# Pooled attention and a gated MLP on one core: the order of all queues made by a list scheduler, and every other early score tile emptied whole

## The chip, the cores and the metric

The kernel runs on one core of a Trainium2 chip. Its time is device microseconds (us) of one execution. The engines are named as the profile names them: PE (matmul; PEld is its weight load), DVE (VectorE), ACT (ScalarE), POOL (GpSimd), SP (the queue that issues all DMAs here). Each engine takes its instructions in the order in which they stand in its queue, and an instruction that waits holds everything behind it on that engine.

## The reference

```python
# q, k, v: (4, 8, 1152, 64) f32;  w_in: (512, 2048), w_out: (2048, 512)
q_pool = q.reshape(B, H, S // 2, 2, D).mean(axis=3)          # 576 pooled queries
scores = matmul(q_pool, k.transpose(0, 1, 3, 2)) / sqrt(D)   # 576 x 1152 per head
attn = exp(scores - max(scores)); attn /= sum(attn) + 1e-9
x = matmul(attn, v)              # -> 2304 tokens x 512
h = x @ w_in
out = (h * clip(h + 3, 0, 6) / 6) @ w_out
```

## The kernel before, in words

**Attention.** The 32 heads are worked in 16 pairs `g`. Of a pair, the pooled queries make 9 score tiles of 128 rows: one that holds the 64 odd rows of both heads, `(None, 0)`, and four per head. Over all there are 144 score tiles `i`. For each tile, `scores` (L229) makes three PSUM tiles `pqk` of 128 x 384 (two matmuls each: an upper and a lower part of q, `qh` and `ql`, against `kT`), and each is emptied by one DVE instruction (L243) that scales it, writes it to the SBUF tile `s` and carries on the running minimum in `cm`. Then `expo` (ACT, L251, 1152 columns, sum in `den`), `recip` (POOL adds eps to `den`, L256; DVE reciprocal, L257), `normal` (POOL, L261, 1152 columns), and `turn` (L263): nine PE transposes into three PSUM tiles `ptp`, each emptied by ACT (L284) or DVE (L282) into `pt`. When the tiles of a row group are turned (5 tiles of 320 columns, then 4 of 256), `values` (L286) multiplies with `vr` into `pav`, and `spill` splits the result into `xh` and `xl` and writes both to DRAM (`xh_d`, `xl_d`).

**Preparation of a pair.** `load_kq`, `load_v`, `pool_q` (L192), `split_k` (L197, L199), `prep_k` (L208, L211, L213), `prep_q` (L221, L226, L227). For pairs after the first, the elementwise part is on POOL.

**Weights.** Of the MLP's weights there are 16 slices `f`, each in two halves (`w_in`, `w_out`). `convert` (L326) rounds a half in seven steps: ACT L331, POOL L332, DVE L334, L338, L341, POOL L344, L345, then a DMA to DRAM (`w_d`, L346). Both halves leave through one staging place, `scratch[:, 0:2]`.

**MLP.** 2304 tokens: six chunks of 256 run among the attention, 16 steps `m` each: `hidden` (12 matmuls `ph`, L88, then L91, L92, L95, L96 on ACT and DVE) and `project` (6 matmuls `po`, L104). Each step loads its slice of the weights from `w_d` again. The last 768 tokens are done behind the attention, as one part of 256 (`mxmxh`, `mxmxl`) and one of 512 (`mxa`, `mxb`): 16 steps of 12 + 6 + 12 + 12 matmuls, the tail.

**What sets the order.** A plan of slots: `at(slot, ...)` files each step under a slot number counted in thirds of a score tile (tile `i` begins in slot 3i; `TRN = 8` slots later it is turned; step `m` of the MLP begins in slot 126 + 6m for the first chunk, then every 2.8 slots). The functions are called in that order, and the framework that turns them into a program lays the instructions of each queue out by an order of its own. PSUM: `pqk` 2 buffers, `ptp` and the other transposes 2, `pav` 1, `ph` 1, `po` 2. The MLP's three buffers are held from the start.

## Time and profile before

| | |
|---|---|
| median of three runs | 1043.81 us (1041.64 to 1047.19) |
| the profiled execution's own time | 1044.61 us |
| its span, first to last instruction | 1042.8 us |
| PE busy | 978.3 us, 94% |
| DVE, ACT, POOL busy | 576.0, 532.3, 426.2 us (55%, 51%, 41%) |
| mean granted TensorE clock | 0.981 |
| DMA | 204 MB, mean 196 GB/s |

A busy PE is an upper bound on its work: matmuls overlap in the array, their ends are modelled, and one that waits for its neighbour looks long. The share is also an average over stages that are limited by different things, so the rows below are taken by stage.

### The profile page before, as it was taken

What the parts mean: (1) busy time and instruction counts of PE and PEld (TensorE: products, weight loads), DVE (VectorE), ACT (ScalarE), POOL (GpSimd) and SP (SyncE); (2) the same over time, 40 slices, a digit from 0 to 9 for tenths busy, and PEclk for the clock granted to TensorE, in tenths of its full rate; (3) what the DMA queues carried; (4) which work ended last, traced back from release to release, by engine and by line L of the source; (5) the groups of instructions that cost most, each with busy time, mean ns of one, the idle gap of its engine ahead of it and who ended that gap; (6) DMA issues with size and microseconds to landing.
All of it is one profiled execution on the core that took longest, in us unless ns stands there. A gap on an engine that the chain in (4) does not pass through costs nothing.

```text
span 1042.8 us, 17686 instructions
## 1 busy us (share of the span) xinstructions
PE 978.3 (94%) x6288; PEld 791.0 (76%) x6288; DVE 576.0 (55%) x1664; ACT 532.3 (51%) x1094; POOL 426.2 (41%) x510
## 2 busy tenths in 40 slices
PE   5797978898899999999999999999999999899997
PEld 3555555566678788888889888888888888688886
DVE  5777666777666656555556554546655454222222
ACT  3555655665465556645556454555555554222222
POOL 4878776878562535342525242342522221000000
PEclk9988989999999999999999999999999999999999
DMA  7665454667754446766767567668656556843332
GB/s 236 207 210 190 171 160 140 214 194 240 235 180 152 154 139 198 226 207 206 262 213 253 183 222 246 199 226 267 225 182 201 194 198 211 298 132 131 122 121 81
DMA packets 80312, 204.06 MB, mean 196 GB/s; under 512 B 7264, under 2 KB 30816, under 8 KB 80224
## 3 DMA queue, kind: packets, MB, share of 16 engines
q1 hardware_dynamic: 80224, 202.93, 59.9%
q8 instruction: 50, 0.82, 0.3%
q14 instruction: 38, 0.31, 0.1%
HBM read 171.97 MB, written 30.93 MB: 195 GB/s over the span
## 4 chain that ended last, share of the span: by engine, by line
PE 76%; POOL 11%; DVE 4%; ACT 3%; issue 2%; DMA 2%; SPq 0%; POOLq 0%; DVEq 0%; ACTq 0%
PE ph L88 18%; PE pqk L239 13%; PE po L104 12%; PE pav L292 12%; PE ptp L269 11%; PE pt L104 6%; POOL s L261 3%; POOL qp L192 2%; POOL scratch L345 2%; PE ptk L208 2%; PE ptq L221 1%; DVE scratch L338 1%; POOL ks L199 1%; DVE s L243 1%; POOL scratch L344 1%
## 5 line engine op out<-in xcount | busy, mean ns | idle before, releaser
L243 DVE TENSOR_SCALAR_CACHE_REDUCE s<-pqk,cm 128x384 f32<-128x384 f32 x288 | 176.5, 613 | 108.0 <-PE pqk L239 105.9
L269 PE MATMUL ptp<-ident,s 128*128 128x128 f32 x1296 | 220.3, 281 | 12.2 <-ACT kT L213 2.2
L261 POOL TENSOR_SCALAR s<-s,den 128x1152 f32<-128x1152 f32 x144 | 181.8, 1263 | 94.6 <-DVE den L257 79.3
L239 PE MATMUL pqk<-kT,qh 128*128 128x384 f32 x480 | 187.4, 406 | 28.1 <-DVE s L243 26.6
L284 ACT COPY pt<-ptp 128x384 f32<-128x384 f32 x314 | 149.0, 480 | 118.4 <-PE ptp L269 113.6
L269 PEld LDWEIGHTS ptp<-ident,s 128*128 128x128 f32 x1296 | 163.9, 144 | 48.4 <-ACT pt L284 9.8
L251 ACT ACTIVATE s<-s,cm 128x1152 f32<-128x1152 f32 x144 | 181.6, 1261 | 27.6 <-DVE s L243 26.5
L88 PE MATMUL ph<-mxmxh,w 128*128 128x256 f32 x896 | 188.6, 292 | 1.1 <-DVE r L92 1.1
L292 PE MATMUL pav<-pt,vr 128*64 128x256 f32 (+1 forms) x1152 | 166.0, 417 | 0.0
L239 PE MATMUL pqk<-kT,ql 128*128 128x384 f32 x480 | 161.7, 353 | 0.0
L256 POOL TENSOR_SCALAR den<-den 128x1 f32<-128x1 f32 x144 | 30.7, 213 | 297.5 <-ACT s L251 291.9
L88 PEld LDWEIGHTS ph<-mxmxh,w 128*128 128x128 f32 x896 | 147.2, 190 | 2.6 <-DVE r L92 1.3
L239 PEld LDWEIGHTS pqk<-kT,qh 128*128 128x128 f32 x480 | 91.4, 197 | 56.3 <-DVE s L243 38.4
L91 ACT ACTIVATE r<-ph,three 128x256 f32<-128x256 f32 (+1 forms) x128 | 63.9, 499 | 133.8 <-PE ph L88 133.6
L88 PE MATMUL ph<-mxmxl,w 128*128 128x256 f32 x448 | 126.9, 283 | 0.0
L292 PEld LDWEIGHTS pav<-pt,vr 128*64 128x64 f32 x1152 | 80.4, 138 | 60.5 <-issue 14.4
L104 PE MATMUL po<-w,gh 128*128 128x512 f32 x384 | 122.8, 397 | 0.0
L92 DVE SCALAR_TENSOR_TENSOR r<-r,ph 128x256 f32<-128x256 f32 (+1 forms) x128 | 57.9, 452 | 111.4 <-ACT r L91 111.2
L243 DVE TENSOR_SCALAR_CACHE_REDUCE s<-pqk 128x384 f32<-128x384 f32 x144 | 79.5, 552 | 41.7 <-PE pqk L239 40.0
L239 PEld LDWEIGHTS pqk<-kT,ql 128*128 128x128 f32 x480 | 94.6, 199 | 2.1
L88 PEld LDWEIGHTS ph<-mxmxl,w 128*128 128x128 f32 x448 | 85.4, 191 | 0.5
L95 ACT CAST gh<-r 128x256 fp32r<-128x256 f32 (+1 forms) x128 | 55.3, 432 | 57.7 <-DVE r L92 56.8
(56 smaller groups left out, 1269.6 us busy)
## 6 DMA issues: line engine op xcount, KB each, us to landing
w<-w_d SPq DMA_DIRECT2D x224, 512.0 KB, 4.7
w_d<-scratch SPq DMA_DIRECT2D x32, 512.0 KB, 3.3
vr<-in_v_dram SPq DMA_DIRECT2D x16, 576.0 KB, 4.5
qr<-in_q_dram SPq DMA_DIRECT2D x15, 576.0 KB, 4.8
kr<-in_k_dram SPq DMA_DIRECT2D x15, 576.0 KB, 4.2
raw<-in_moe_w_in_dram SPq DMA_DIRECT2D x16, 512.0 KB, 4.1
raw<-in_moe_w_out_dram SPq DMA_DIRECT2D x16, 512.0 KB, 3.8
mxmxh<-xh_d SPq DMA_DIRECT2D x7, 512.0 KB, 5.7
```

Source lines behind the costliest of these rows:

```text
L88: nc.tensor.matmul(ps, w[:, wi, cs], x[:, c, o:o + n], start=(m == 0), stop=(m == 3 * NCC - 1))
L91: nc.scalar.activation(out=r6, in_=ps, func=AF.Relu, bias=three)
L92: nc.vector.scalar_tensor_tensor(out=r6, in0=r6, scalar=6.0, in1=ps, op0=ALU.min, op1=ALU.mult)
L95: nc.scalar.copy(out=gh, in_=r6)
L104: nc.tensor.matmul(o, g[:, ts], w[:, wi, :], start=(f == 0 and n == 0), stop=(f == NFC - 1 and n == 2))
L239: nc.tensor.matmul(ps, x, kk.rearrange("p t k -> p (t k)"), start=(m == 0), stop=(m == len(ops) - 1))
L243: nc.vector.tensor_scalar(out=s_t[i][:, c * NK:(c + 1) * NK], in0=ps, scalar1=-SCALE, scalar2=cm_t[i][:, c - 1:c] if c else None, op0=ALU. ...
L251: nc.scalar.activation(out=s, in_=s, func=AF.Exp, bias=cm_t.pop(i)[:, 2:3], scale=-1.0, accum_out=den)
L261: nc.gpsimd.tensor_scalar(out=s, in0=s, scalar1=den_t.pop(i), scalar2=1.0, op0=ALU.mult, op1=ALU.mult)
L269: nc.tensor.transpose(ps[:, x, :], s_t[i][:, o:o + P], ident)
L284: nc.scalar.copy(out=to, in_=ps)
L292: nc.tensor.matmul(av[j * D:(j + 1) * D, :], vr_t[g][:, j, t, :], pt_t[g, gr][:, t, j, :], start=(t == 0), stop=(t == KT - 1),)
```

## The change

The plan of slots is gone. Each step is filed with `add(key, place, cost, fn, needs, takes, frees)`: a place (the old slot numbers, a little shifted), a cost in ns on each engine that may do it, the steps that it needs, the buffers that it takes and frees. `Order.run` walks through time: whenever an engine is free it takes, of the steps that are ready and whose buffers have room, the one with the smallest place. Where a step names two engines (evictions of transposes on ACT or DVE; steps of `convert` and of the preparation on POOL or on DVE/ACT), the one that is free first takes it, the second engine with a handicap in place. The resulting order is then forced on every queue by dependencies without a semaphore. The loops are cut into finer steps (loads, pooling and splitting by head; `hidden` in five). The numbers also change: a tile is turned 7 slots after its scores (8 before), the MLP begins at place 112 with 6.4 per step (126 and 6), `project` follows 1 place behind (4), a slice of the weights every 12.5 (13).

Two edits change instructions. In tiles `i < 40` with even `i`, all three score parts go into one PSUM tile `pw` of three banks and are emptied by one DVE instruction of 1152 columns; those three banks are the ones that `ph` and `po` take afterwards. And eps is added to `den` on DVE instead of POOL.

```diff
-EXP, REC, NRM, TRN = 2, 5, 5, 8
-FIRST, STEPS, LAG = 126, (6, 2.8), 4
-CONV, CSTEP = 6, 13
-ALONE = 40
+REC, NRM, TRN = 4, 4.5, 7
+FIRST, STEPS, LAG = 112, (6.4, 2.8), 1
+CONV, CSTEP = 6, 12.5
+WIDE = 40
+class Order:
+    WAKE = 60
+    def run(self):
...
+        while len(out) < len(steps):
+            back.sort()
+            while back and back[0][0] <= t:
+                room[back.pop(0)[1]] += 1
+            began = False
+            for e in engines:
+                if free[e] > t:
+                    continue
+                best = None
+                for n in wait[e]:
+                    if ready[n] <= t and all(room[b] > 0 for b in steps[n][4]):
+                        place = steps[n][0] + (steps[n][1][e][2] if e != "SP" and len(steps[n][1][e]) > 2 else 0)
+                        if best is None or (place, n) < best:
+                            best = (place, n)
...
+                free[e] = t + busy
...
+        return [(steps[n][2], e) for _, n, e in out]
...
+        def whole(i):
+            return i < WIDE and i % 2 == 0
+
+        def scores(eng, i, c):
...
+            if whole(i):
+                if c == 0:
+                    ps_t[i] = ps_w.tile([P, KT // KC, 512], F32, tag="w", name="pw")
+                ps = ps_t[i][:, c, 0:NK]
+            else:
+                ps = ps_t[i, c] = ps_s.tile([P, NK], F32, tag="s", name="pqk")
...
+        def least(eng, i, c):
...
+            if whole(i):
+                nc.vector.tensor_scalar(
+                    out=s.rearrange("p (c k) -> p c k", c=KT // KC), in0=ps_t.pop(i)[:, :, 0:NK],
+                    scalar1=-SCALE, scalar2=None, op0=ALU.mult, op1=ALU.min, accum_out=cm[:, c:c + 1],
+                )
...
-            nc.gpsimd.tensor_scalar(out=den, in0=den, scalar1=1.0, scalar2=EPS, op0=ALU.mult, op1=ALU.add)
+            nc.vector.tensor_scalar(out=den, in0=den, scalar1=EPS, scalar2=None, op0=ALU.add)
             nc.vector.reciprocal(out=den, in_=den)
...
+        room = dict(kr=2, qr=2, qp=2, ks=1, vr=2, tr=2, kT=12, w=1, s=2, S=5, pt0=1, pt1=1, av=1, xo=2,
+                    raw0=1, raw1=1, size0=1, size1=1, wd=1, mx=2, w0=3, w1=3, h=1, r6=2, g=3, o0=1, o1=1, ob=2)
+        MOVE = {"ACT": (400, 480), "DVE": (480, 555, 1.5)}
...
+                    add(("tp", i, c), z + TRN + c, {"PE": (330, 550)}, partial(turn, i=i, c=c),
...
+                    add(("ev", i, c), z + TRN + c, MOVE, partial(take, i=i, c=c), [("tp", i, c)], (), ("tr",))
+                add(("ex", i), z + 3, {"ACT": (1270, 1460)}, partial(expo, i=i), [("cp", i, 2)])
+                add(("rc", i), z + REC, {"DVE": (280, 340)}, partial(recip, i=i), [("ex", i)])
+                add(("nm", i), z + NRM, {"POOL": (1340, 1360)}, partial(normal, i=i), [("rc", i)])
...
+        COSTS = ({"ACT": (580, 680)}, {"POOL": (630, 660), "DVE": (340, 420, 3)}, {"DVE": (430, 500)}, {"DVE": (700, 780)},
+                 {"DVE": (700, 780)}, {"POOL": (650, 720), "ACT": (580, 680, 3)}, {"POOL": (1340, 1350), "DVE": (700, 780, 6)})
...
+                add(("lr", f, h), z - 8, {"SP": (470, 3000, 1550)}, partial(load_raw, f=f, half=h), [("mm", 0, 2)], (f"raw{h}",))
...
+        add(("second",), 3 * WIDE, {"SP": (1, 1, 0)}, lambda eng: second_part(), [("cp", i, 2) for i in range(WIDE)])
...
+        for fn, eng in [(lambda eng: None, None)] + od.run():
+            fn(eng)
+            for ins in nc.cur_bb.bb.instructions[done:]:
+                if ins.engine in before:
+                    tc.add_manual_dep(ins, before[ins.engine].name, queue, reason="order")
+                before[ins.engine] = ins
```

Three places in the queues follow. The first is the beginning of ACT's queue. `ks<-kr` is the upper part of k, `kT<-ptk` and `qh<-ptq` empty PE's transposes of k and q, `scratch<-raw` is the first step of `convert`, `s<-s,cm` is the exponential. Before:

```order
L197 CAST ks<-kr 128x9x64
L213 COPY kT<-ptk 128x384
L331 ACTIVATE scratch<-raw 128x512
L213 COPY kT<-ptk 128x384
L197 CAST ks<-kr 128x9x64
L226 CAST qh_122<-ptq 128x64
L226 CAST qh_122<-ptq 128x224
L213 COPY kT<-ptk 128x384 x2
L331 ACTIVATE scratch<-raw 128x512
```

and of the change:

```order
L395 ACTIVATE s,den<-s,cm 128x1152 x2
L483 ACTIVATE scratch<-raw 128x512
L303 COPY kT<-ptk 128x384
L349 CAST qh_125<-ptq 128x288
L483 ACTIVATE scratch<-raw 128x512
```

The first `scratch<-raw` stood second among the evictions of the first pair; now it stands behind all of the first pair's and behind two exponentials.

The second place is POOL's queue at the first normalizations (`s<-s,den`). Before:

```order
L256 TENSOR_SCALAR den<-den 128x1
L332 TENSOR_SCALAR scratch<-scratch 128x512
L261 TENSOR_SCALAR s<-s,den 128x1152
L256 TENSOR_SCALAR den<-den 128x1
L261 TENSOR_SCALAR s<-s,den 128x1152
L344 CAST scratch<-scratch 128x512
L345 TENSOR_TENSOR scratch<-scratch 128x512
```

and of the change:

```order
L406 TENSOR_SCALAR s<-s,den 128x1152
L502 TENSOR_TENSOR scratch<-scratch 128x512
L406 TENSOR_SCALAR s<-s,den 128x1152
L485 TENSOR_SCALAR scratch<-scratch 128x512
L406 TENSOR_SCALAR s<-s,den 128x1152
L305 CAST scratch<-scratch 128x512
```

The one-column instruction ahead of each normalization is gone from POOL, and some steps of `convert` with it (they stand on DVE or ACT).

The third place is SP's queue at the end of the attention. `xh_d<-xh` and `xl_d<-xl` are the last spills; `mxmxh`, `mxmxl`, `mxa`, `mxb` are the tail's inputs. Before, with the loads of weights between:

```order
L307 DMA xh_d<-xh 128x320
L308 DMA xl_d<-xl 128x320
L70 DMA w_10190<-w_d 128x1024
L77 DMA mxmxh<-xh_d 128x4x256
L70 DMA w_10274<-w_d 128x1024
L70 DMA w_10244<-w_d 128x1024
L70 DMA w_10319<-w_d 128x1024
L77 DMA mxmxl<-xl_d 128x4x256
```

and of the change:

```order
L461 DMA xh_d<-xh 128x256
L461 DMA xl_d<-xl 128x256
L160 DMA mxmxh<-xh_d 128x4x256
L160 DMA mxmxl<-xl_d 128x4x256
L160 DMA mxa<-xh_d 128x4x512
L160 DMA mxb<-xl_d 128x4x512
```

Before, the first part's inputs were loaded behind the spill of 320 columns, one row group ahead of the last; now all four loads stand behind the last spill, of 256 columns.

## Rows read from the trace of the kernel before

**Rows 1.** From the page: the clock granted to TensorE in 40 equal slices of 26 us, in tenths of full speed.
```profile
PEclk9988989999999999999999999999999999999999
```

**Rows 2.** Busy time by stretch: from:to in us, its length, then busy us of PE, PEld, DVE, ACT and POOL (with the count of instructions that began there), granted clock, DMA share, GB/s.
```profile
0.00:25.00 25.00, 13.57 (x50) 9.75 (x50) 14.70 (x42) 9.30 (x18) 10.08 (x16) 1.00 0.79 246
...
41.00:238.00 197.00, 168.26 (x969) 110.63 (x967) 140.22 (x368) 115.89 (x238) 153.55 (x173) 0.92 0.56 185
...
400.00:850.00 450.00, 448.99 (x3154) 381.44 (x3153) 246.27 (x772) 242.15 (x509) 150.43 (x190) 1.00 0.67 217
...
234.00:895.00 661.00, 648.43 (x4538) 546.65 (x4538) 373.80 (x1157) 360.92 (x755) 252.15 (x310) 0.99 0.65 211
895.00:1043.00 148.00, 137.69 (x696) 116.66 (x696) 39.62 (x71) 38.60 (x71) 0.00 (x0) 1.00 0.41 134
```

**Rows 3.** The chain that ended last, in pieces (start us, us, what), from stretches where PE never rests: the price of each kind of PE work. `pav` x36 are the records of one row group's 18 matmuls. The last two are from the tail and one step of it apart.
```profile
514.50 5.00 PE pav L292 x36
...
600.29 4.04 PE pav L292 x36
...
607.11 0.38 PE pqk L239 x2
607.49 0.33 PE ptp L269 x3
607.82 1.44 PE ph L88 x12
...
610.84 1.39 PE po L104 x6
...
922.66 2.72 PE ph L88 x12
...
930.92 2.72 PE ph L88 x12
```

**Rows 4.** Groups of PE's instructions in 41 to 238 us (line, engine, operation, out<-in, shape, count | busy us, mean ns of one | idle time before them and what ended it).
```profile
L269 PE MATMUL ptp<-ident,s 128*128 128x128 f32 x324 | 58.5, 297 | 10.4 <-ACT pt L284 1.9 <-ACT kT L213 1.9 <-POOL den L256 1.8
L239 PE MATMUL pqk<-kT,qh 128*128 128x384 f32 x116 | 48.5, 434 | 16.1 <-DVE s L243 15.9
...
L292 PE MATMUL pav<-pt,vr 128*64 128x320 f32 x144 | 31.0, 476 | 0.0
```

**Rows 5.** The same view of the same stretch: groups on DVE and POOL.
```profile
L243 DVE TENSOR_SCALAR_CACHE_REDUCE s<-pqk,cm 128x384 f32<-128x384 f32 x70 | 42.8, 611 | 13.6 <-PE pqk L239 12.8
...
L345 POOL TENSOR_TENSOR scratch<-scratch 128x512 fp32r<-128x512 f32 x23 | 31.4, 1366 | 1.5
...
L338 DVE SCALAR_TENSOR_TENSOR scratch<-raw,scratch 128x512 uint32<-128x512 uint32 x24 | 26.4, 1102 | 0.4
...
L341 DVE SCALAR_TENSOR_TENSOR scratch<-raw,scratch 128x512 uint32<-128x512 uint32 x24 | 22.3, 928 | 0.3
...
L243 DVE TENSOR_SCALAR_CACHE_REDUCE s<-pqk 128x384 f32<-128x384 f32 x35 | 19.2, 549 | 0.7
L344 POOL CAST scratch<-scratch 128x512 fp32r<-128x512 f32 x24 | 17.9, 748 | 6.6 <-DMA w_d<-scratch 4.6 <-DVE s L243 1.7
...
L256 POOL TENSOR_SCALAR den<-den 128x1 f32<-128x1 f32 x36 | 9.5, 264 | 15.7 <-ACT s L251 13.7
...
L282 DVE COPY pt<-ptp 128x384 f32<-128x384 f32 x12 | 6.6, 551 | 0.1
...
L257 DVE RECIPROCAL den<-den 128x1 f32<-128x1 f32 x36 | 5.8, 160 | 25.6 <-POOL den L256 25.4
...
L227 DVE TENSOR_TENSOR ql<-ptq,qh 128x288 fp32r<-128x288 f32 x8 | 3.6, 453 | 0.6 <-ACT qh L226 0.4
...
L227 DVE TENSOR_TENSOR ql<-ptq,qh 128x64 fp32r<-128x64 f32 x8 | 1.7, 214 | 0.0
```

**Rows 6.** All executions of line 338: count, shortest, median and longest in ns, start of the first and the last in us.
```profile
L338 DVE SCALAR_TENSOR_TENSOR scratch<-raw,scratch x32: 679/980/1789, 12.5 to 282.6; 128x512 uint32<-128x512 uint32 x32
```

**Rows 7.** Who waited for whom in 41 to 238 us: waiting engine and line <- awaited: us in total, times, longest.
```profile
PEld pqk L239 <- DVE s L243: 23.5, 23, 2.8
PE pqk L239 <- DVE s L243: 15.9, 14, 2.2
```

**Rows 8.** The chain that ended last, in the first 45 us (start us, us, what).
```profile
3.06 6.86 DMA raw<-in_moe_w_in_dram
...
18.68 4.34 POOL qp L192 x4
```

**Rows 9.** The passage into the tail: instructions in order of time (start us, us, what, in brackets the idle time before it and what ended it); the last row is the time from issue to landing of `mxa`'s load.
```profile
890.79 4.11 PE L292 MATMUL pav<-pt,vr 128*64 128x256 f32 x36
...
897.11 0.37 SPq L77 DMA_DIRECT2D mxa<-xh_d  x1
...
910.00 0.50 PE L88 MATMUL ph<-mxb,w 128*128 128x512 f32 x1 [1.73 <-DMA mxb<-xl_d]
...
DMA to landing us min/median/max: 7.8/7.8/7.8
```

**Rows 10.** The MLP's first matmul and the weights' way through DRAM: count, shortest, median, longest in ns, start of the first and the last in us; the last row is the time from issue to landing of the DMAs of L346.
```profile
L88 PE MATMUL ph<-mxmxh,w x896: 277/283/561, 234.2 to 1020.1; 128*128 128x256 f32 x180
...
L346 SPq DMA_DIRECT2D w_d<-scratch x32: 319/326/497, 16.1 to 287.3; - x32
...
DMA to landing us min/median/max: 2.6/3.3/6.6
```

More of the change, by code (lines that the diff above doesn't have):

```diff
@@ L1 @@
 from contextlib import ExitStack
+from functools import partial
 import numpy as _np
@@ L229, in scores, with tiles, pair, load_k @@
-        def scores(i, c):
-            g, n = divmod(i, NTI)
-            j, t = TILES[n]
-            ps = ps_s.tile([P, NK], F32, tag="s", name="pqk")
+        def tiles(g):
+            return TILES if g else EARLY
+        kr_t, vr_t, ks_t, kT, qr_t, qp_t, tr_t = {}, {}, {}, {}, {}, {}, {}
+        ps_t, s_t, cm_t, den_t, pt_t, av_t, xo_t = {}, {}, {}, {}, {}, {}, {}
+        def pair(g, j):
+            b, p = divmod(g, NPAIR)
+            return b, 2 * p + j
+        def load_k(eng, g, j):
+            b, h = pair(g, j)
+            kr_t[g, j] = ld.tile([P, KT, D], F32, tag="kr", name="kr")
+            nc.sync.dma_start(out=kr_t[g, j], in_=k[b, h].rearrange("(p t) d -> p t d", p=P))
@@ new lines, in load_q, with load_v @@
+        def load_q(eng, g, j):
+            b, h = pair(g, j)
+            qr_t[g, j] = ld.tile([QP, QT, 2, D], F32, tag="qr", name="qr")
+            nc.sync.dma_start(out=qr_t[g, j], in_=q[b, h].rearrange("(p t r) d -> p t r d", p=QP, r=2))
+        def load_v(eng, g):
+            b, h = pair(g, 0)
+            vr_t[g] = vp.tile([P, 2, KT, D], F32, tag="vr", name="vr")
+            nc.sync.dma_start(out=vr_t[g], in_=v[b, h:h + 2].rearrange("h (p t) d -> p h t d", p=P))
+        by = {"DVE": nc.vector, "POOL": nc.gpsimd}
@@ new lines, in take_q @@
+        def take_q(eng, g, j, half):
+            qh, ql = q_t[g % 2]
+            ps = tr_t["q", g, j, half]
+            for c0, c1, to in QPARTS[half]:
+                to = to or REST * j
+                o = slice(to, to + c1 - c0)
+                if eng == "ACT":
+                    nc.scalar.copy(out=qh[:, j, o], in_=ps[:, c0:c1])
+                else:
+                    nc.vector.tensor_tensor(
+                        out=ql[:, j, o], in0=ps[:, c0:c1], in1=qh[:, j, o].bitcast(F32), op=ALU.subtract
+                    )
@@ L271, in turn, with take @@
                 s_t.pop(i)
-            gr = 0 if j is None or t < 2 else 1
-            if n in (0, 5) and c == 0:
+            if (g, gr) not in pt_t:
                 pt_t[g, gr] = tp.tile([P, KT, 2, GROUPS[gr][1]], F32, tag=f"pt{gr}", name=f"pt{gr}")
+        def take(eng, i, c):
+            g, gr = group(i)
+            j, t = tiles(g)[i % NTI]
+            ps = tr_t.pop(("p", i, c))
             to = pt_t[g, gr][:, KC * c:KC * (c + 1)]
@@ L297, in spill, with split_x @@
-        def spill(g, gr):
+            for t in range(t0, t1):
+                for j in range(2):
+                    nc.tensor.matmul(
+                        av[j * D:(j + 1) * D, :], vr_t[g][:, j, t, :], pt_t[g, gr][:, t, j, :],
+                        start=(t == 0), stop=(t == KT - 1),
+                    )
+        def split_x(eng, g, gr):
+            n = GROUPS[gr][1]
+            if eng == "ACT":
+                xo_t[g, gr] = [xo.tile([P, GROUPS[0][1]], F32R, tag=t, name=t)[:, 0:n] for t in ("xh", "xl")]
+                nc.scalar.copy(out=xo_t[g, gr][0], in_=av_t[g, gr])
+            else:
+                xh, xl = xo_t[g, gr]
+                nc.vector.tensor_tensor(out=xl, in0=av_t.pop((g, gr)), in1=xh.bitcast(F32), op=ALU.subtract)
@@ new lines, in pooled_attention_then_gated_mlp @@
+            for n in range(2):
+                add(("lw", m, n), z - 6 + 2 * n, {"SP": (470, 3500, 1550)}, partial(do_load_w, m=m, n=n), [("sw", f, n)], (f"w{n}",))
+            add(("hd", m), z, {"PE": (1440, 1660)}, partial(do_layer, m=m), [("lw", m, 0), ("lx", c), ("second",)],
+                ("h",), ("w0",) + (("mx",) if f == NFC - 1 else ()))
+            add(("re", m), z, {"ACT": (400, 472)}, partial(do_relu, m=m), [("hd", m)], ("r6",))
+            add(("ga", m), z, {"DVE": (340, 418)}, partial(do_gate, m=m), [("re", m)], (), ("h",))
@@ L448, in pooled_attention_then_gated_mlp @@
                 if 0 <= f < NFC:
[L449 to L451 removed]
+                    w = parts[n][1]
+                    g = hidden(gt if n else gp, ph[n].tile([P, DM], F32, tag="h", name="ph")[:, 0:w], xs[n], w_t[f, 0], w)
                     pend.append((n, g, f))
```

513 lines of the change are left out of this document (308 added, 205 removed).

## The prediction, made before the changed kernel was run

> **What bounds the kernel now.** I read the page's clock row and the stretches first, because the page's one number (PE 94% busy) is a mean over stages. In 400 to 850 us PE is busy 449.0 of 450 us, and no other engine is over 55% [rows 2]: this stage is PE's, and an order of the queues can give little there. In 41 to 238 us the shares are PE 168, POOL 154, DVE 140, ACT 116 of 197 us [rows 2]. No engine is full, and the granted clock dips below full speed only in this part [rows 1], a mean of 0.92 [rows 2].
>
> PE's 168 us overstate its work. The chain of the full stage gives prices: a pair of score matmuls 0.38 us, three transposes 0.33, the value matmuls of a row group 5.00 or 4.04, twelve `ph` 1.44, six `po` 1.39 [rows 3]. In 41 to 238 us there are 324 records of score transposes, 116 pairs of score matmuls, and four row groups of 320 columns (144 records at 36 each) [rows 4], by the program as many of 256; at these prices 35.6 + 44.1 + 36.2 us, and some 10 us for the transposes of q and k (24 sets and 16 sets of three by the program, at no more than 0.33 us: at most 13). That is 126 us of work in 197, or 64%. So some 70 us are lost here, and the reader should see them as waits between engines: the wait rows show score matmuls waiting for DVE to empty the two `pqk` buffers, 23.5 us on the weight load and 15.9 on the matmul [rows 7].
>
> In 41 to 238 us, 35 score tiles go through (35 first parts on L243 [rows 5]): 5.6 us each.
>
> **The early stretch, engine by engine.** The change redistributes work, and I counted instructions on each queue between the normalization of tile 4 and that of tile 40, before and after.
>
> DVE: the 36 tiles have three L243 each before. One of 384 columns takes 0.549 us when it is the first and 0.611 after [rows 5], so 1.77 us a tile. In the change 18 of the 36 are one instruction of 1152 columns, which no row shows. Its price is bounded by three first parts, 1.65 us, from above; from below, by DVE's own slope: 64 columns take 0.214 us and 288 take 0.453 [rows 5], 1.07 ns a column, so 0.549 + 768 x 0.00107 = 1.37 us. I take 1.4, since the slope is DVE's own: 18 x 0.37 = 7 us less. (At 1.65 it is 2 us less.) Nine of the 48 instructions L338 and L341 move past the mark, at 1.10 and 0.93 us: 9 us less; two L334 more, 1 us. The eps addition moves to DVE, 36 times; one column of the reciprocal takes 0.160 us there and the addition took 0.264 on POOL [rows 5]; at 0.16, 6 us more (9.5 at most). Evictions of transposed scores on DVE go from 12 to 36, at 0.551 us: 13 us more. Seven steps come over from POOL's preparation and `convert`, at some 0.6 us: 4 us. Sum: 140 - 7 - 9 + 1 + 6 + 13 + 4 = **148 us**.
>
> POOL loses 36 additions (9.5 us), 7 of L345 (9.6), 16 of L344 (12.0) [rows 5] and some 20 us of other steps: from 154 to about 102. ACT loses 24 evictions and gains 11 conversions: some 5 us less, about 111. PE keeps its 126. So DVE becomes the fullest engine, and 148 us is the floor for these 35 tiles if DVE never waits; the present 197 is the ceiling if the chain of waits stays.
>
> Here a rule speaks against the change. Lines 338 and 341 read two SBUF operands, and line 338 takes 0.679 us at its shortest and 1.789 at its longest [rows 6]: they are stretched when POOL works. The Trainium skill, "Perfetto Trace Analysis", section "Optimizing Scalar/DVE Operations", says that GpSimd and DVE share an SBUF read port, so that moving work between the two might not help. If they excluded each other outright, the stretch would need 148 + 102 = 250 us, 53 more than now. The row denies that strong form: DVE and POOL were busy 140 + 154 = 294 us within 197 [rows 2].
>
> How full can DVE be? The fullest engine now reaches 78% here (POOL, 154 of 197) under an order by slots, and 100% (PE) where the order fits [rows 2]. The new order is made with costs close to these rows (an eviction on DVE is 0.555 us in it and 0.551 here), knows the buffers, and POOL, which stretches DVE, is a third emptier. I take 94%: 148 / 0.94 = 157 us. **Term: -40** (at 100%, -49; at 78%, -7; nothing if chains bound it).
>
> **The start.** Now ACT's second eviction of transposed k stands behind the first step of `convert`, whose data land only after 6.86 us on the path; then four steps of POOL's pooling for the second pair, 4.34 us, stand ahead of the first normalization [rows 8]. In the change that `convert` step is behind two exponentials, and the first score tile needs one head instead of two. What takes the place: DVE's own work for the first tiles, and POOL's queue still has three pooling steps ahead of its first normalization. Bounds 0 and 11.2; I take 8. **Term: -8.**
>
> **The middle, from the first `ph` (234 us [rows 10]) to the last values (about 895 us [rows 9]).** PE is busy 648.4 of 661 us [rows 2]. An order can give back the 12.6 us of idle time and part of the low clock; it can also lose some in a forced queue. MLP steps are filed as filler, so that the order of the change reaches `m` = 15 at tile 57 instead of 70. Bounds 0 and -13. **Term: -7.**
>
> **The end.** From 895 us on, 148 us pass with 137.7 of PE [rows 2]; a step of the tail is 930.92 - 922.66 = 8.26 us [rows 3] and stays as it is. Before, the first part's inputs are loaded ahead of the last spill, and 4.2 us of leftover MLP work (12 `ph` and two times 6 `po`) follow the last values. In the change all MLP steps stand ahead of the last values and all four loads behind the last spill. After the last values (4.11 us from 890.79), `mxa` was issued at 897.11 and took 7.8 us [rows 9]; a load half its size now goes out about there, and a second behind it. I take 6 us of waiting for it, then some for `mxb`, in place of the three waits of now, of which the longest is 1.73 us [rows 9]. **Term: +3** (bounds 0 and +7).
>
> **Sum.** 1044.6 - 40 - 8 - 7 + 3 = 992.6 us, on the profiled execution's own time (0.8 us above the median, which is inside the spread of the runs): **992 us**. This is a gain of 5%. A measurement of this kernel tells about 0.5% (5 us) from no change.
>
> **Rivals.**
>
> *The early stretch stays bound by its chains.* DVE is idle 57 of 197 us now with everything it needs somewhere else. One instruction for three score parts cannot start before the third matmul: the last value of the tile is out 1.4 us after it, not 0.61 [rows 5]. For it: PE's waits for DVE [rows 7]. Against: in the order of the change other matmuls stand between the parts, so that PE has work meanwhile. If nothing is gained in the stretch: 1044.6 - 8 - 7 + 3 = 1033. If the longer emptying comes on top, 20 x 0.8 = 16 us, 1049 at the worst, around no change. The Trainium skill's page just named says, in the same section, that where DVE and ACT are not saturated and cause bubbles elsewhere, breaking instructions up may let work finish sooner. The trace agrees on the premise (DVE at 71% with PE waiting for it); no run here shows yet what follows.
>
> *The weights come late: slower.* The MLP's first 16 steps now follow close on the weights that they need, and `ph` at the head of PE's queue holds scores and transposes behind it. Both halves of a slice leave through one staging place, held over L344, L345 and the DMA: 0.75 + 1.37 + 3.3 = 5.4 us at least [rows 5, 10]. Now the 32 halves take 16 to 287 us, 8.8 each [rows 10]. In the forecast tile 40 is at 238 - 48 = 190 us. Up to `m` = 15 PE then has 15 steps of 2.83 us and 17 tiles of 126 / 35 = 3.6 us, 104 us, so it comes at 294 us; with 10 us for the last landing and load, 32 halves have from some 12 to 284 us: 8.5 us each. Each us more per half costs PE 32 us; slower than now is reached at 8.5 + 52 / 32 = 10.1 us a half. Against it: conversions have POOL at 65% instead of 78%, and two engines may do three of the seven steps. For it: a write's landing goes up to 6.6 us [rows 10].
>
> *Better than forecast.* DVE at 100% (-49), the start -11, the middle -13, the end 0: 971; if POOL's lighter load also takes the stretch out of L338 and L341 (39 x 0.35 = 14 us), under 960.
>
> **Chances and range.** The forecast's own band, 962 to 1022: 0.70. Faster than that 0.07. Chain-bound, 1022 to 1038: 0.11, of it the half up to 1026. Whole tiles eat the gain, no change: 0.05. Weights late, slower: 0.07. The range 962 to 1026 holds what is wanted. Faster 0.88, same 0.05, slower 0.07.
>
> **What the profile after would show.** Right: the first `ph` near 187 us instead of 234; between tiles 5 and 40 DVE over 90% busy and POOL near 65%; hardly a slice under full clock after the first few; whole tiles at 1.3 to 1.5 us; 400 us to the last values at PE 100% as now; a single wait of 5 to 8 us ahead of the tail. Wrong: DVE still near 75% with waits for PE and ACT (chains), PE waiting under `ph` for loads of `w` or for `w_d` (weights), L338 longer than its present mean of 1.10 us (port), or new gaps in PE after 400 us (forced order).

## The result, and the profile after

The changed kernel takes **1007.6 us** (median of four runs, 1004.2 to 1009.8) against 1044.2 for the kernel before: a ratio of **0.965, 95% interval 0.961 to 0.969**. 992 was forecast, in a range of 962 to 1026. The profiled execution took 1009.1 us, with a span of 1007.1.

The stretches cut at the same events as in [rows 2]: the reciprocal of tile 5 (31 us; 41 before) to that of tile 40 (192; 238 before), from the first `ph` (192 too; 234 before) to the end of the last values (857; 895 before), and the rest. Columns as in [rows 2]; the second row is the first part of the third.

```profile
31.00:192.00 161.00, 137.58 (x923) 99.78 (x923) 151.41 (x349) 106.28 (x212) 108.61 (x93) 0.97 0.59 195
192.00:330.00 138.00, 125.40 (x862) 104.68 (x861) 110.44 (x303) 81.09 (x170) 63.91 (x58) 0.98 0.81 261
192.00:857.00 665.00, 650.17 (x4568) 551.58 (x4566) 428.42 (x1312) 368.13 (x770) 215.22 (x185) 0.99 0.68 220
857.00:1007.00 150.00, 136.81 (x672) 116.50 (x672) 38.01 (x68) 36.67 (x68) 0.00 (x0) 0.95 0.39 127
```

The same lengths, to a tenth of a us by the times at which these instructions start and end:

| part | forecast | before | after | measured |
|---|---|---|---|---|
| start, to tile 5 | -8 | 41.2 | 30.7 | -10.6 |
| tiles 5 to 40 | -40 | 196.7 | 160.9 | -35.8 |
| middle, first `ph` to last values | -7 | 660.7 | 664.6 | +3.9 |
| end | +3 | 147.9 | 150.5 | +2.6 |

The measured parts sum to -39.9, the forecast's to -52; the span got shorter by 35.7 us. The 4 us between come from where the parts meet: before, the first `ph` starts 3.7 us ahead of the reciprocal of tile 40, so that the middle overlaps the stretch ahead of it, and now it starts 0.4 us behind it. Counted from tile 40, the middle takes 665.1 us instead of 657.0, 8 us more. All that was gained is gained by 192 us; the middle, which was to give some more, takes some back.

DVE is busy 151 of 161 us in the early stretch, 94%, where 148 at 94% was forecast, and POOL 67% (65% was). DVE's costliest groups there (compare [rows 5]; L496 and L492 are the old L341 and L338, L487 the old L334):

```profile
L381 DVE TENSOR_SCALAR_CACHE_REDUCE s<-pw 128x1152 f32<-128x1152 f32 x17 | 22.9, 1349 | 0.3 <-PE pw L373 0.2
L496 DVE SCALAR_TENSOR_TENSOR scratch<-raw,scratch 128x512 uint32<-128x512 uint32 x19 | 21.4, 1124 | 0.1
L386 DVE TENSOR_SCALAR_CACHE_REDUCE s<-pqk,cm 128x384 f32<-128x384 f32 x35 | 21.2, 606 | 0.8 <-PE pqk L373 0.8
L305 DVE COPY pt<-ptp 128x384 f32<-128x384 f32 x34 | 18.5, 551 | 2.0 <-PE ptp L417 1.4
L487 DVE TENSOR_SCALAR scratch<-scratch 128x512 uint32<-128x512 uint32 x19 | 18.2, 955 | 2.4 <-POOL scratch L485 2.3
L492 DVE SCALAR_TENSOR_TENSOR scratch<-raw,scratch 128x512 uint32<-128x512 uint32 x19 | 17.3, 911 | 0.2
...
L401 DVE TENSOR_SCALAR den<-den 128x1 f32<-128x1 f32 x35 | 5.0, 144 | 1.6 <-ACT s L395 1.3
...
PE ptp L417 <- DVE pt L305: 8.1, 6, 2.9
```

The last row is from the list of waits: PE's longest wait in this stretch is now for DVE's evictions of transposed scores, 8.1 us where it was 1.5 before.

The prices that no row of before showed were sized well: a whole tile at 1.349 us (1.4 taken), the addition at 0.144 (0.16 taken), 34 evictions (36 counted).

In the middle, the first 138 us hold nearly all of PE's idle time: 12.6 us, and from 330 to 850 us hardly 2. Before, the first 138 us of the middle held 10.8:

```profile
234.00:372.00 138.00, 127.23 (x874) 104.85 (x874) 89.82 (x271) 79.69 (x163) 78.17 (x92) 0.98 0.59 189
```

So the idle time that the order was to give back is still there. Who waits for the weights in these 138 us, and all writes of converted weights (L505; 16.1 to 287.3 us and 3.3 us to landing in the median before [rows 10]):

```profile
ACT scratch L303 <- DMA w_d<-scratch: 14.9, 7, 4.0
POOL scratch L305 <- DMA w_d<-scratch: 9.8, 3, 4.8
...
PE po L203 <- DMA w<-w_d: 2.5, 2, 1.6
...
L505 SPq DMA_DIRECT2D w_d<-scratch x32: 319/327/807, 28.4 to 306.6; - x32
...
DMA to landing us min/median/max: 2.6/4.9/9.9
```

PE itself waits little for weights; its 12.6 us are spread over many waits, none over 3.5 us in total. But the steps that need the weights come thinly: the second `ph` step starts 12 us after the first.

At the end, PE waits for the tail's first load, and then runs at half clock. First the wait, from the list of waits from 855 us on; then stretches of 5 us (the columns as above):

```profile
PE ph L170 <- DMA mxmxh<-xh_d: 6.0, 1, 6.0
...
855.00:860.00 5.00, 1.60 (x16) 0.78 (x12) 0.42 (x1) 0.37 (x1) 0.00 (x0) 0.98 0.79 234
860.00:865.00 5.00, 1.60 (x5) 1.31 (x6) 0.00 (x0) 0.00 (x0) 0.00 (x0) 0.50 0.99 323
865.00:870.00 5.00, 3.92 (x18) 3.63 (x18) 0.85 (x2) 0.88 (x2) 0.00 (x0) 0.50 0.75 284
```

### The profile page after: what moved, and what is told of

It is laid out like the page before. It is cut to its first block, busy times and chain, and to the rows that moved or that the text cites. A ratio compares the mean times of both kernels' runs of the same rounds, so it can differ in the third digit from the quotient of the medians.

```text
span 1007.1 us, 17813 instructions
## 1 busy us (share of the span) xinstructions
PE 946.6 (94%) x6288; PEld 786.0 (78%) x6288; DVE 643.2 (64%) x1799; ACT 532.0 (53%) x1092; POOL 341.9 (34%) x297
## 4 chain that ended last, share of the span: by engine, by line
PE 73%; DVE 14%; DMA 8%; issue 2%; ACT 2%; POOL 1%; SPq 1%; POOLq 0%; ACTq 0%
PE ph L170 19%; PE po L203 15%; PE pqk L373 11%; PE ptp L417 11%; PE pav L442 10%; PE pt L203 4%; DMA w_d<-scratch 4%; DVE s L386 3%; DVE scratch L487 2%; DVE scratch L496 2%; DVE pt L305 1%; PE ptk L327 1%; DVE s L381 1%; DVE scratch L492 1%; DVE gl L188 1%
## 5 line engine op out<-in xcount | busy, mean ns | idle before, releaser
L303 ACT COPY pt<-ptp 128x384 f32<-128x384 f32 x279 | 132.0, 479 | 94.4 <-PE ptp L417 92.5
L386 DVE TENSOR_SCALAR_CACHE_REDUCE s<-pqk,cm 128x384 f32<-128x384 f32 x248 | 150.5, 610 | 31.9 <-PE pqk L373 29.8
L373 PE MATMUL pqk<-kT,qh 128*128 128x384 f32 x411 | 157.2, 398 | 2.2 <-DVE s L386 2.2
L203 PE MATMUL po<-w,gh 128*128 128x512 f32 x448 | 142.2, 399 | 0.0
L373 PE MATMUL pqk<-kT,ql 128*128 128x384 f32 x411 | 133.0, 339 | 0.0
L305 DVE COPY pt<-ptp 128x384 f32<-128x384 f32 x153 | 84.3, 554 | 58.5 <-PE ptp L417 57.6
L203 PE MATMUL po<-w,gl 128*128 128x512 f32 x224 | 94.5, 422 | 5.3 <-DMA w<-w_d 2.5
L203 PEld LDWEIGHTS po<-w,gh 128*128 128x128 f32 x448 | 86.0, 192 | 15.1
L188 DVE TENSOR_TENSOR gl<-r,gh 128x256 fp32r<-128x256 f32 (+1 forms) x128 | 78.0, 610 | 26.0 <-ACT gh L183 25.6
L373 PEld LDWEIGHTS pqk<-kT,qh 128*128 128x128 f32 x411 | 76.0, 191 | 6.8 <-DVE s L386 5.0
```

What stands on the lines that cost most here:

```text
L188: nc.vector.tensor_tensor(out=gl, in0=r6, in1=gh.bitcast(F32), op=ALU.subtract)
L203: nc.tensor.matmul(o, g[:, ts], w[:, wi, :], start=(f == 0 and n == 0), stop=(f == NFC - 1 and n == 2))
L303: nc.scalar.copy(out=out, in_=in_)
L305: by[eng].tensor_copy(out=out, in_=in_)
L373: nc.tensor.matmul(ps, x, kk.rearrange("p t k -> p (t k)"), start=(m == 0), stop=(m == len(ops) - 1))
L386: nc.vector.tensor_scalar(out=s[:, c * NK:(c + 1) * NK], in0=ps_t.pop((i, c)), scalar1=-SCALE, scalar2=cm[:, c - 1:c] if c else None, op0= ...
```

## The experiments

Two theories stood at the start. **DVE:** DVE's work is the floor of the early stretch, as the forecast had it, and every us taken from it comes back. **Weights:** the first pass of the MLP waits for the conversions, so what is won early is partly lost behind 192 us. The rivals are chains of waits, and that each difference comes from a reshuffled order. The runs of before beside the experiments have medians of 1043.2 to 1044.2 us, so medians can be set beside 1007.6; below some 4 us (the runs of one kernel differ by 2 to 6) a difference is not resolved.

Each kernel has one profile, of one of its runs, and places of events in it have a spread of their own. Three profiles are in the same order up to 196 us: the changed kernel's and those of two experiments below, the one with all weight slices at hand and the one on the passage into the tail. In them the first `ph` comes at 192.0, 192.2 and 190.6 us, and DVE is busy 151.4, 147.8 and 148.2 us between 31 and 192. So a shift of under 2 us in such a place is not resolved either. "Step 16" below is the first MLP step of the second chunk, `m` = 16; the first pass ends with the step ahead of it.

### What the whole tiles give

```diff
 def whole(i):
-    return i < WIDE and i % 2 == 0
+    return False
```

> The new order stays, made anew with three emptyings of 384 columns for every early score tile; the second edit is taken out. Theory (the early stretch is bound by DVE's work): 20 tiles cost DVE 0.549 + 2 x 0.611 = 1.77 us each instead of 1.349, 8.4 us in all, so the reciprocal of tile 40 comes at about 200 us instead of 192, DVE stays over 90% busy from tile 5 to 40, and the time is 6 to 8 us above the changed kernel's 1007.6. Rival (chains bind it): the last value of a whole tile is out 0.8 us later than with three parts, so that taking it out gives 5 to 16 us back and the time falls below 1003. A third reading: the three banks of a whole tile are above all one more buffer for PE, and without them PE waits for DVE again: more than 12 us slower.

Measured: 1009.3 us, ratio 0.967 (0.965 to 0.969). The first `ph` comes at 199.7 us instead of 192.0, as the theory had it, but the end only 1.6 us later, which is not resolved. So whole tiles go with some 8 us up to tile 40 and with nothing that is resolved in all; nearly all of the gain is there without them. The middle makes up for the later start: PE is busy 131.6 us between 192 and 330 instead of 125.4. Two things keep this from being more exact: the order is another one, and the banks of `pw` are also one more buffer. PE's waits for score buffers from 31 to 192 us, first with whole tiles, then (last row) without:

```profile
PE pw L373 <- DVE s L381: 3.0, 6, 0.8
PE pqk L373 <- DVE s L386: 0.7, 2, 0.4
...
PE pqk L373 <- DVE s L386: 10.2, 11, 2.5
```

How much of the 8 us is DVE's work and how much this buffer stays open.

### Without the addition

```diff
-            nc.vector.tensor_scalar(out=den, in0=den, scalar1=EPS, scalar2=None, op0=ALU.add)
...
-                add(("rc", i), z + REC, {"DVE": (280, 340)}, partial(recip, i=i), [("ex", i)])
+                add(("rc", i), z + REC, {"DVE": (100, 160)}, partial(recip, i=i), [("ex", i)])
```

> Leaves out the addition of 1e-9 to the sum of exponentials (that sum is at least 1, so in 32 bits the addition changes nothing). Theory (DVE's work binds the early stretch): 41 additions at 0.144 us, 0.18 with the wait between two dependent instructions, are 6 to 7 us of DVE, so the reciprocal of tile 40 comes at 185 to 186 us instead of 192 and the time falls by 4 to 7 us, to 1001 to 1004. If the chain of one tile bound it, the same 0.18 us would only be shortened once per passage of the chain and tile 40 would come at 190 or later: less than 2 us. If the weights set the pace behind tile 40, tile 40 comes early and the 16th step of the MLP does not: about 0 to 3 us.

Measured: 1005.0 us, 0.963 (0.960 to 0.966): 2.6 us, not resolved. That is the time of the third reading, but tile 40 is not early as it would have it (its reciprocal at 191.1 us, 191.6 in the changed kernel), nor is the first `ph` (194.4 us): with another cost the scheduler made another order. This run says little on DVE.

### All weight slices at hand

```diff
-            w_t[m, n] = load_w(wp, m % NFC, n)
+            w_t[m, n] = load_w(wp, m % NFC if m >= NFC else 0, n)
...
-[("sw", f, n)]
+[("sw", f if m >= NFC else 0, n)]
```

> Leaves out that the first pass of the MLP (the first 256 rows) uses its own 16 weight slices: each of its steps loads slice 0, which is converted by 20 us or so, as many bytes as before; all conversions still take place. Theory (the middle lost its forecast 7 us because the first pass follows the conversions, one staging place and writes that take 6.3 to 7.5 us to land): PE's 12.6 us of idle time between 192 and 330 us mostly go, step 16 comes 8 to 12 us earlier than 327 us, and the time falls by 6 to 12 us to 996 to 1002. Rival (the idle time there is PE waiting for evictions on ACT and DVE, which only takes its turn as the last wait): idle stays over 8 us and the time stays within 3 us of 1007.6.

Measured: 999.2 us, 0.957 (0.954 to 0.960), 8.4 us less. The early stretch is as in the changed kernel, whose order every queue keeps up to 196 us (first `ph` at 192.2); behind it the second and third steps follow within 8 us, not 24, and PE's busy time from 192 to 330 us grows by the gain:

```profile
192.00:330.00 138.00, 133.17 (x935) 110.71 (x932) 114.21 (x333) 85.74 (x179) 76.45 (x68) 0.99 0.73 251
```

One part of the expectation failed: step 16 comes at 344 us, not at 315 to 319. The first steps run sooner, attention gets the time behind them (tile 54 at 277 us instead of 295), and the order of both is another. A step's time is no measure where the order may change; that the gain lies where the theory puts it is what this run shows, and how much of it is the new order's it does not.

### The passage into the tail

```diff
 add(("hd", m), z, ..., [("lw", m, 0), ("lx", c), ("second",)]
+    + ([("av", NG - 1, 1, 0)] if m >= NFC * len(chunks) - 3 else []),
...
 add(("sd", c, t), ..., [("so", c, t)]
+    + ([("ll",)] if c == len(chunks) - 1 else []),
...
-add(("lx", len(chunks)), z, ..., every, ("mx",))
+add(("lx", len(chunks)), z0 + 26, ..., spills(NT - TAIL, NT - TAIL + CT), ("mx",))
```

> The last spill's passage is undone in part: the inputs of the first tail part are loaded once the spills that they need are through (ahead of the last one), three steps of the MLP (8.5 us) are held until the last values, and the last two output writes go behind the tail's loads. Theory (the end costs what PE waits for the first loads of the tail, 7.2 us, with a granted clock of 0.64 from 855 to 872 us): nearly all of the wait goes, the clock stays at 1.0, and the time falls by 6 to 10 us to 998 to 1002. Rival: the held steps keep their weight buffers, the tail's own weights come late instead, and the wait only changes its name: within 3 us of 1007.6.

Measured: 1002.3 us, 0.960 (0.958 to 0.962), 5.3 us less, a little under what was expected. Every queue is in the changed kernel's order up to 840 us, so no reshuffled order ahead of the passage is in this difference. The wait for `mxmxh` is gone from the list of waits, and in the same place PE is busy and at full clock:

```profile
860.00:865.00 5.00, 5.00 (x26) 4.05 (x25) 1.67 (x4) 1.79 (x4) 0.00 (x0) 1.00 0.87 260
865.00:870.00 5.00, 3.48 (x22) 2.80 (x21) 1.24 (x2) 0.68 (x2) 0.00 (x0) 1.00 0.93 340
```

What is left of the loss has moved ahead of the last values, where PE now lacks the held steps (8.9 of 10 us busy from 845 us on; 10.0 in the changed kernel).

### Two staging places, with an order of their own

```diff
-w = scratch[:, 0:2, :]
+w = scratch[:, 2 * half:2 * half + 2, :]
...
-room: wd=1, xo=2
+room: wd0=1, wd1=1, xo=1
```

> The conversions' two halves get a staging place each (4 KB more a partition, paid for with one buffer instead of two for the values on their way out); the order is made anew. Theory (the first pass of the MLP is held back by the conversions, and those by the one staging place that stays taken while its write of 5 us lands): the waits of ACT and POOL for the write of converted weights, 25 us between 192 and 330 us, go; step 16 comes earlier than 327 us and the time falls by 4 to 8 us, towards the 999 that the kernel with all slices at hand took. Rival (the conversions are late because DVE is full through 290 us, their five DVE steps wait their turn): within 3 us of 1007.6, and the waits for the write turn into waits for DVE.

Measured: 999.9 us, 0.958 (0.955 to 0.961), 7.8 us less, at the upper end. But the order is another too (the first `ph` at 199.1 us, 7 later; the last step of the first pass at 313.6, 7.6 sooner; step 16, expected ahead of 327, at 332), so which of the two gave the gain this run alone does not tell.

### Evictions to ACT

```diff
-MOVE = {"ACT": (400, 480), "DVE": (480, 555, 1.5)}
+MOVE = {"ACT": (400, 480), "DVE": (480, 555, 4)}
```

> One number in the order's costs is changed: an eviction of transposed scores or k goes to DVE only when it is 4 places more urgent (1.5 before), so that most of the 42 such copies on DVE between tiles 5 and 40 (0.55 us each) go to ACT (0.40 to 0.48 us), which is busy 106 of 161 us there. Theory (DVE's work binds the early stretch, and through its conversion steps the weights too): DVE has up to 20 us less to do, the stretch gets 8 to 15 us shorter and the time falls by 4 to 12 us. Rival (chains: PE waits for the evictions themselves, which on one engine stand behind exponentials of 1.3 us): PE's waits for ACT's copies grow beyond the present 8 us, and the time is the same or up to 5 us longer.

Measured: 1001.3 us, 0.958 (0.955 to 0.962), 6.3 us less, and yet inconclusive: the work hardly moved. DVE still has 32 evictions of scores in the early stretch (34 in the changed kernel), and 172 of scores and k in all (180); why no more went to ACT was not looked into. **A handicap that moves 8 of DVE's 180 copies, two of them in the early stretch, changed the time by 6 us**, with another order of everything else. So a difference of this size between two orders proves no cause, and the next three runs keep the order of every queue as it is.

### One staging place or two, in the same order

Two places as above; the scheduler still counts `wd=1, xo=2`, so that the queues are those of the changed kernel, instruction by instruction.

> The two staging places of the earlier run, now in the changed kernel's own order, instruction by instruction (the scheduler still counts one place; the buffers are two, and one instead of two for the values on their way out). So no reshuffled order is in this difference. Theory (one staging place, taken while its write lands, holds the first pass of the MLP back): the waits for the write of converted weights go; the first matmul of the MLP stays near 190 to 192 us, step 16 comes at 318 to 323 us instead of 327, and the time falls by 4 to 8 us. Rival (the 8 us that two places gave with an order of their own came from that order; in the old queues the same instructions wait for DVE and POOL instead): less than 3 us.

Measured: 1002.2 us (five runs, 998.3 to 1003.3), 0.959 (0.957 to 0.962): 5.4 us less. ACT's and POOL's waits for the write, 18.1 and 12.3 us between 31 and 330 us, are gone. But much of the gain falls ahead of the MLP, where the theory had none: the first `ph` comes at 188.6 us (-3.4), step 16 at 321 (-6.7), as forecast. PE's waits for the loads grow, from 2.5 us to 6.0:

```profile
PE po L203 <- DMA w<-w_d: 6.0, 4, 3.1
```

The one place costs some 5 us over both stretches together; behind it the loads are next.

### Less work for DVE, in the same order

```diff
 elif step == 3:
-    nc.vector.scalar_tensor_tensor(out=t, in0=low, scalar=29, in1=t, op0=ALU.logical_shift_right, op1=ALU.bitwise_or)
+    pass
```

> Leaves out one of the conversions' DVE steps, L492, which puts the low word's three bits into the weights (they are then cut and not rounded there); the order of everything else is that of the changed kernel, instruction by instruction. Theory (DVE's work binds the early stretch): 19 of these steps at 0.911 us lie between 31 and 192 us, 17 us of 151; the first matmul of the MLP comes at 174 to 180 us instead of 192, and the time falls by 10 to 16 us. Rival (the chains of one score tile bind it, and DVE is full because its stretched instructions fill the gaps): the first matmul of the MLP comes at 187 us or later, and the time falls by less than 6 us.

Measured: 996.9 us, 0.955 (0.953 to 0.957), 10.8 us less: the time is the theory's, the place is the rival's. The first `ph` comes at 189.2 us, 2.8 sooner (1.4 to 3.0 by the three profiles named above), though 17.3 us of DVE's work are gone ahead of it. Step 16 comes 9.0 us sooner, at 318.5. (This profile is of the slowest run, 1000.3 us.) DVE falls to 87% of the stretch:

```profile
31.00:192.00 161.00, 140.46 (x945) 102.10 (x944) 140.50 (x338) 108.90 (x219) 105.85 (x94) 0.97 0.60 202
```

What is waited for instead is the write of the weights: POOL in the early stretch in this kernel, below, where the same wait was 2.5 us in the changed kernel. From 192 to 330 us PE gains 4.6 us, 130.0 for 125.4.

```profile
POOL scratch L305 <- DMA w_d<-scratch: 9.4, 3, 6.6
```

So DVE's 94% is not a floor of which each us counts; it is one of several limits that lie close together. And most of what the lighter DVE gives comes behind the first `ph`, where the weights are needed: their last half leaves at 298.6 us, not 306.6.

### Less work for POOL, in the same order

```diff
-nc.gpsimd.tensor_scalar(out=s, in0=s, scalar1=den_t.pop(i), ...)
+nc.gpsimd.tensor_scalar(out=s[:, 0:S // 2], in0=s[:, 0:S // 2], scalar1=den_t.pop(i), ...)
```

> Leaves out half of POOL's normalization (the first 576 of 1152 columns are normalized, the others not), in the changed kernel's order. POOL has 35 x 0.7 = 25 us less to do between 31 and 192 us. Theory (DVE's conversion steps are stretched by POOL: L487 takes 0.41 us when POOL stands and 0.955 in the mean, L496 0.69 and 1.124): their means fall, L496 below 1.0 and L487 below 0.8, DVE's work falls by 6 to 12 us, the first matmul of the MLP comes at 180 to 187 us and the time falls by 4 to 10 us. Rival (the chain: each tile's values are out 0.7 us sooner): the means of L487 and L496 stay, and the stretch gets shorter all the same. Third: neither, the first matmul of the MLP within 3 us of 192.

Measured: 995.1 us, 0.952 (0.950 to 0.955), 12.5 us less, more than expected, with the first `ph` at 185.5 us and step 16 at 316.5 (-11.0). DVE's conversion steps, whose work is the same, get shorter; L487 stays a little above the 800 that was named. In the changed kernel the means of L487, L496 and L492 were 955, 1124 and 911 ns, in the two other profiles of this order 908, 987 and 840, and 884, 1015 and 888:

```profile
L487 DVE TENSOR_SCALAR scratch<-scratch 128x512 uint32<-128x512 uint32 x20 | 16.7, 834 | 1.8 <-POOL scratch L485 1.5
L496 DVE SCALAR_TENSOR_TENSOR scratch<-raw,scratch 128x512 uint32<-128x512 uint32 x19 | 16.1, 849 | 0.1
L492 DVE SCALAR_TENSOR_TENSOR scratch<-raw,scratch 128x512 uint32<-128x512 uint32 x19 | 15.2, 799 | 0.2
```

That POOL stretches DVE is shown, since all three means lie below all three of these; its size is less sure. At the changed kernel's means these 58 would take 9.8 us more (20 x 0.955 + 19 x 1.124 + 19 x 0.911 = 57.8, against 48.0), at those of the two other profiles 5 to 6. DVE's busy time falls by 5.9 (by 2 to 3 against the others), in a stretch that also takes in more. How much of the 6.5 us to the first `ph` is this, and how much the shorter way of each tile (0.54 us in POOL's mean), stays open.

### All together

The first three edits of these (no addition, two places with their own order, the passage), with a fourth held step:

```diff
+    + ([("tp", NTI * NG - 1, 2)] if m == NFC * len(chunks) - 4 else [])
```

> Three edits at once: no addition of 1e-9, a staging place for each half, and the changed passage into the tail, there with a fourth held step that may run before the last values. If what each gives is taken from a different wait: 2.6 from the addition, 5 to 7 from the passage, 4 to 8 from the second staging place, so 990 to 996. If the second staging place gives nothing (DVE full): 998 to 1001.

Measured: 1001.3 us, 0.960 (0.958 to 0.962). The gains do not add: the three together give no more than the second staging place alone gave. With the evictions' handicap of 4 as well:

> The same three edits and the evictions moved to ACT as well. If DVE's work is what binds until the weights are done: another 4 to 10 us less than without them, 982 to 992. If the evictions on ACT lengthen the chains: the same or up to 5 us more than without them.

Measured: 993.8 us, 0.953 (0.950 to 0.955). By the run on evictions, this difference too may be the order's alone. The last kernel has all four edits too; in it five held steps stand behind stages of the last two tiles (not in the diff below), and the MLP is spread:

```diff
-FIRST, STEPS, LAG = 112, (6.4, 2.8), 1
+FIRST, STEPS, LAG = 112, (6.4, 2.95), 1
```

> The four edits of the fastest so far (no addition, two staging places, evictions on DVE only when 4 places more urgent, the changed passage into the tail), and the last steps of the MLP spread: filed 2.95 places apart instead of 2.8, the last three still behind the last values, the five ahead of them behind stages of the last two tiles. If PE still loses some 6 us around the last tiles for lack of other work, 987 to 991; if the spacing only moves the loss, within 2 us of 993.8.

Measured: **989.6 us** (988.3 to 991.1), 0.948 (0.947 to 0.950), faster than both kernels. The last half of the weights leaves at 269.7 us, not 306.6, PE is busy 134.9 of the 138 us from 192 on (125.4), and at the passage the clock stays up:

```profile
L504 SPq DMA_DIRECT2D w_d<-scratch x32: 319/326/1067, 29.8 to 269.7; - x32
...
192.00:330.00 138.00, 134.90 (x960) 113.50 (x961) 112.23 (x305) 87.96 (x182) 61.87 (x55) 0.99 0.73 245
...
845.00:860.00 15.00, 13.18 (x73) 11.01 (x73) 3.92 (x8) 4.15 (x8) 0.00 (x0) 1.00 0.81 277
860.00:875.00 15.00, 15.00 (x79) 12.88 (x78) 4.72 (x9) 4.39 (x8) 0.00 (x0) 1.00 0.41 132
```

## Why the prediction was right, and where not

**The early stretch (-40, measured -36): right in size, half right in its reason.** The count of DVE's work was close (148; 151 measured, 148 in the two other profiles of this order) and the change did end PE's waits for the two score buffers: for 15.9 us on the matmul [rows 7] the same list of after shows 3.7 (3.0 for whole tiles, 0.7 for `pqk`). The rival that chains hold the stretch at 197 us fell with the result. But the step "148 us is the floor" and then 94% of it takes DVE for the only limit. With 17 us less to do in the same queues the stretch gave 2.8; with POOL's normalization halved 6.5; with a second staging place 3.4. None of them alone is the bound; that 94% came out is partly chance.

**The port.** The forecast denied the strong form of the rule, since DVE and POOL were busy 294 us within 197 [rows 2]. That sum cannot deny it for a part of DVE's instructions. The two lines of evictions into `s`, which read PSUM, are not stretched; the three conversion lines, from SBUF to SBUF, are (section on the hardware). The forecast's best case, in which a lighter POOL also takes the stretch out, did not come: POOL is busy 67% instead of 78%, yet the two lines that it named take as long together as before (L338 1.102 us in the mean, now 0.911 as L492; L341 0.928, now 1.124 as L496), and L334, 630 ns in 41 to 238 us, rose to 955 as L487 (884 and 908 in the two other profiles): 19 x 0.25 to 0.33 = 5 to 6 us. So the sign that was to tell of the port, a mean of L338 above 1.10 us, did not show, and the waiting was in the other two lines.

**The start (-8, measured -10.6)** was inside its bounds; no run takes its parts asunder.

**The middle (-7, measured +4, or +8 from tile 40 on) is the step that failed.** It let the order give back idle time, and named the late weights only as a rival with a price for "slower". The mechanism of that rival was at work all the time at a smaller size: a half leaves every 9.0 us (32 from 28.4 to 306.6 us; 8.7 before), no faster than before, although the MLP starts 42 us sooner. The forecast's own sum left 8.5 us a half, named 8.8 as the pace of before, and priced each us more at 32 us of PE's time; it still booked nothing for the gap, because it took a lighter POOL for a faster pace. At 9.0 that sum gives 16 us of lateness. That is more than was lost, since PE had other work in the meantime: `m` = 15 starts at 321 us, not at 294, but PE is idle only 12.6 us between 192 and 330. With slices at hand the kernel takes 8.4 us less, with a second place in the same order 5.4. In the three runs that keep the order (two places, less DVE, less POOL) the gain by the first `ph` is 3.4, 2.8 and 6.5 us, and by step 16 it is 6.7, 9.0 and 11.0, with the last half of the weights leaving 7 to 9 us sooner: 3 to 6 us of each are gained behind the first `ph`, where the first pass needs the weights. How the middle's 8 us divide between the weights and the other waits, no run tells.

**The end (+3, measured +2.6)** was right in its wait (5 to 8 us; 6.0 on PE's matmul, 6.4 and 1.1 on its weight load for the two inputs). That the granted clock would be halved behind it was not foreseen, so that the size agrees is in part luck; without both, 5.3 us come back.

**The whole tiles** were priced right in DVE's time (7 us forecast). The 7.7 us by which the first `ph` is later without them agree with it, but may be the buffer's in part; to the end they are worth nothing that is resolved, because the middle takes it back.

## What to carry to other kernels

A term for one stage is a gain only if the next stage can take it: when a stage starts 40 us sooner, ask first what it consumes (here converted weights at 9 us a half), and count that on the same clock. A busy share of 94% on one engine does not make it the bound when its own instructions are stretched by a neighbour; take work out in an unchanged order and look where the time appears. And where a scheduler makes the order, a cost edited by a hair reshuffles it: here that was worth 6 us with hardly any work moved, so causes are tested with the order held, and versions are picked by time.

## What the runs showed of the hardware

**A DVE instruction from SBUF to SBUF can stand still while POOL works.** All executions of three DVE lines in the changed kernel (count, shortest, median, longest in ns; L386 in the early stretch only):

```profile
L487 DVE TENSOR_SCALAR scratch<-scratch x32: 407/427/3743, 21.1 to 298.5; 128x512 uint32<-128x512 uint32 x32
L496 DVE SCALAR_TENSOR_TENSOR scratch<-raw,scratch x32: 673/842/2360, 23.6 to 303.8; 128x512 uint32<-128x512 uint32 x32
L386 DVE TENSOR_SCALAR_CACHE_REDUCE s<-pqk,cm x35: 598/605/618, 31.2 to 188.0; 128x384 f32<-128x384 f32 x35
```

L386 reads its tile from PSUM and stays within 20 ns, whatever POOL does. The 15 executions of L487 with no POOL instruction beside them take 407 to 428 ns; the 13 that take over 600 all have one beside them. L487 takes nine times its shortest in the longest case, and the timeline shows which (start us, us, what; in brackets the idle time before):

```profile
119.56 1.23 POOL L406 TENSOR_SCALAR s<-s,den 128x1152 f32<-128x1152 f32 x1
...
119.94 3.74 DVE L487 TENSOR_SCALAR scratch<-scratch 128x512 uint32<-128x512 uint32 x1
...
120.75 1.29 POOL L502 TENSOR_TENSOR scratch<-scratch 128x512 fp32r<-128x512 f32 x1
...
121.98 1.41 POOL L319 TENSOR_TENSOR ks<-kr,ks 128x576 fp32r<-128x576 f32 x1
...
123.60 0.55 DVE L305 COPY pt<-ptp 128x384 f32<-128x384 f32 x1
...
124.29 0.52 PE L417 MATMUL ptp<-ident,s 128*128 128x128 f32 x3 [2.91 <-DVE pt L305]
```

It begins while a POOL instruction runs and ends 0.29 us after the third one in a row (121.98 + 1.41 = 123.39; spans on POOL are rough), and the eviction queued behind it keeps PE waiting for 2.9 us. The same execution takes 3.74 to 3.75 us in all five profiles of this order in which POOL's work is whole. With the normalization halved, the first of the three POOL instructions is 0.49 us shorter, and L487's longest is 0.47 us shorter:

```profile
L487 DVE TENSOR_SCALAR scratch<-scratch x32: 407/427/3275, 21.9 to 287.9; 128x512 uint32<-128x512 uint32 x32
```

The Trainium skill, "SBUF — State Buffer", section "SBUF: two separate sides", has DVE and GpSimd share a port pair as a lock that one of them holds for a whole instruction, against DVE's instructions with two SBUF inputs or in a two-port mode. This trace agrees, in that L492 and L496, with two SBUF inputs, are stretched and L386, which reads its tile from PSUM, is not; in which mode L487 runs, no run here shows. And POOL began two more instructions while DVE's was under way.

**A wait of 6 us on PE was followed by some 10 us at half clock.** After PE had been busy 1.6 of the 5 us from 855 on, the granted clock is 0.50 from 860 to 870 us (1.2 of 2.4 GHz), 0.83 in the next ten and 1.00 from 880 on; without the wait it is 1.00 from 855 on.
